# Top-32 attention with a phase mixer: the fill of the padded queries, the order of the two heads' value products, two issue orders and the folds' priority are changed

## The chip, the cores and the metric

The kernel runs on one NeuronCore of a Trainium2 chip. The metric is device time in microseconds, from one launch. The core has TensorE (PE in the profile; its weight loads are PEld), VectorE (DVE), ScalarE (ACT), GpSimd (POOL) and SyncE (SP, which here issues all transfers). Each engine works through its own list of instructions in order; a scheduler wrote these lists when the kernel was built, and semaphores tie them together.

## The reference

For 8 batches, 8 heads, 576 positions and head size 64 it computes attention that keeps the 32 largest scores of each query, and feeds the result, 512 channels wide, to a mixer:

```
scores = q @ k.T / 8
kth    = 32nd largest score of each row
attn   = softmax(where(scores >= kth, scores, -1e9))
x      = attn @ v                      # heads side by side: (8, 576, 512)
theta  = x @ w_theta
y      = w_tok_r @ (x * cos(theta)) + w_tok_i @ (x * sin(theta))
u      = x + y
out    = u + relu(u @ w_ch)
```

## The kernel before, in words

The attention is cut into 160 units: 8 batches, 4 pairs of heads each, 5 units a pair. Units j = 0 to 3 of a pair hold 128 queries of both heads; unit j = 4 holds the last 64 queries of both, which a padded tile `qpad` (zeros around two 64-column blocks) brings into one product of 128 rows. One `qpad` tile serves all 32 pairs.

A unit goes through these steps, each a function or a helper of the kernel:

- `scores` (PE L260): products of the split keys (`kh`, `kl`) with the queries into PSUM tile `ps_score` (two of them), then an ACT copy of each to `e` (L269, or L280 for j = 4). For j = 4 it first calls `pad_pair`, which fills `qpad` (L241).
- `fold` (DVE L296 to L299): maxima and minima of one half of the scores against the other; this also frees `ps_score`. `pick` (DVE L304), then `threshold` (DVE L320, L326, L330) find the 32nd largest score; POOL writes the limit `lim` (L331).
- `penalize` (ACT L350, POOL L352) and `exponent` (ACT L362) make the softmax numerators.
- `turn`: PE transposes the numerators (`pt` L377, left-over columns `pq` L387 or L391), ACT copies them to `at` (L379, L382) and `rem` (L388, L394).
- `mix_values`: for every second or so unit (j = 1 and j = 4) PE multiplies by the values into `px`: four key blocks, and in each the two heads, which go to the two halves of the output partitions (L407, 64 columns of weights each; one such product of the code is two rows of the trace), and one product for the left-over keys (L410). ACT copies the result to `xt` (L419).

After the four pairs of a batch comes its mixer, a generator that `turn` advances in small shares, so that its work lies between the next batch's units: transposes `px_s` (PE L603), normalization (DVE L502), transposes `px_t` (PE L517), the phase products `pth` (PE L540, L544), the fraction of a turn (ACT L556, DVE L557), sine and cosine (ACT L564 to L566, which need another ACT table; exponentials load theirs again at L362), the token mixing `py` (PE L656, settled by DVE L632) and the channel products `po` (PE L688, DVE L637, output L639). The last batch's mixer has nothing beside it.

The pipeline takes the steps of neighbouring units in the order PTUFKSTVMXZ, with scores and fold of unit i + 3 ahead of unit i (step S). A Tile scheduler then places every instruction by priority and readiness. Two kinds keep the order in which they are written: those that were given the token "table" (exponentials and sines on ACT) and those with the token "fixed" (on PE: `pt`, `pq` and, through `fill`, the mixer's products of all batches but the last; in the second last one the channel products are free).

At the start the weights are converted from 64-bit floats: loads L145, ACT L156, L157, L159, POOL L158, L160, L161. Each pair's keys and queries are split in two parts by ACT L212 and POOL L213 and spread by twelve transfers (L225). Values come by L232 and L235 (`vrem`, 64x64 a transfer).

Of the kernel before, what the change touches and what calls it, by code (L numbers as in the profile page):

```python
# [9 lines left out]
F32 = mybir.dt.float32  # L10
# [8 lines left out]
P = 128  # L19
# [3 lines left out]
AHEAD = 3  # L23
S_LATE = 0
# [22 lines left out]
def topk_attention_phase_mixer(  # L47
# [11 lines left out]
    nc = tc.nc  # L59
    B, NPAIR, _, S = qT.shape  # L60
    DM = w_ch.shape[0]
    D = P // 2
    H = 2 * NPAIR
    HS = S // 2
    NJ = S // P
# [22 lines left out]
    ident = const.tile([P, P], F32, name="ident")  # L88
# [85 lines left out]
    def later(n):  # L174
        return tc.high_priority(offset=-n)
# [62 lines left out]
    def pad_pair(pr):  # L238
        qpad = qpads[pr["p"] % NQP]
        for a in range(2):  # L240
            nc.scalar.copy(qpad[:, a, a * D : a * D + D], pr["q2"][:, a, NJ * P : S])  # L241
        pr["qpad"] = qpad

    class Unit:
# [152 lines left out]
    def mix_values(u):  # L397
        if u.j not in (1, NJ):
            return
        pr, bt, p = u.pair, u.batch, u.p  # L400
        c = 0 if u.j == 1 else 1
        n, q0 = QN[c], c * QN[0]
        px = ps_m.tile([P, 512], F32, tag="m", name="px")
        for kb in range(NJ):
            for a in range(2):
                sl = slice(a * D, a * D + D)
                nc.tensor.matmul(  # L407
                    px[sl, :n], pr["vt"][:, kb, sl], pr["at"][:, a, kb], start=(kb == 0), stop=False, skip_group_check=True
                )
        nc.tensor.matmul(px[:, :n], pr["vr"], pr["rem"], start=False, stop=True, skip_group_check=True)  # L410
        u.px = px
# [49 lines left out]
    def mixer(bt, split=False, beside=False, parts=False):  # L461
        bq, xt, sums, sums_rem = bt["bq"], bt["xt"], bt["sums"], bt["sums_rem"]
# [134 lines left out]
        for k in range(NJ + 4):  # L597
            if k <= NJ:
                rows = P if k < NJ else REM
                px = ps_t.tile([P, DM], F32, tag="t", name="px_s")  # L600
                with later(M_PE):
                    for p in range(NB):
                        fill(nc.tensor.transpose(px[:rows, p * P : p * P + P], xt[:, p, k * P : k * P + rows], ident))  # L603
                normalize(k, px)
            if 0 <= k - 3 <= NJ:
                fraction(k - 3)
            if 0 <= k - 2 <= NJ:
                angles(k - 2)
                yield TURN * share() / 2
            if 0 <= k - 1 <= NJ:  # L610
                turn_back(k - 1)
            yield TURN * share() / 2 if k <= NJ + 1 else 0
# [56 lines left out]
        for m in range(NB):  # L669
            if not split:  # L670
                ot = wk2.tile([P, S], F32, tag="ot", name="ot", bufs=1)
            else:
                if m % 2 == 0:
                    ots = wk2.tile([P, 2, S], F32, tag="kh", name="ots")
                ot = ots[:, m % 2]
            for c in range(2):
                cs = slice(c * HS, c * HS + HS)
                po = accumulator(m, c, "po")
                ms = slice(m * P, m * P + P)
                if split or parts:  # L680
                    mm = []
                    for kb in range(NB):
                        mm += passes(*(w[kb][:, ms] for w in w_parts["ch"]), u_hi[kb][:, cs], u_lo[kb][:, cs])
                else:
                    mm = [(wts["ch"][kb][:, ms], xt[:, kb, cs]) for kb in range(NB)]
                for i, (l, r) in enumerate(mm):
                    with later(M_TOK if split or parts else 0):
                        ins = nc.tensor.matmul(po[:, :HS], l, r, start=(i == 0), stop=(i == len(mm) - 1))  # L688
                        if not parts:
                            fill(ins)  # L690
                    if not split:
                        yield NB / len(mm)
                        flush()
                late.append(lambda m=m, c=c, cs=cs, o=ot, y=po[:, :HS]: give(m, c, cs, o, y))
                if split:
                    flush()
# [9 lines left out]
    def pipeline():  # L706
        NU = NJ + 1
        wsteps = widen_steps()
        total = B * NPAIR * NU
        units, pairs, batches, running, budget = {}, {}, {}, [], [0.0]  # L710

        def unit(i):
            if not 0 <= i < total:
                return None
            if i not in units:
                g, j = divmod(i, NU)
                b, p = divmod(g, NPAIR)
                if b not in batches:
                    batches[b] = new_batch(b)
                    if b % MARKED:  # L720
                        batches[b]["marks"] = batches[b - 1]["marks"]
                units[i] = Unit(b, batches[b], p, j, pairs[g], (g * (2 * NJ + 1) + 2 * j) % NSLOT, False)
            return units[i]

        def fetch(g):
            if g < B * NPAIR:
                pairs[g] = load_pair(*divmod(g, NPAIR))

        def split(g):
            if g < B * NPAIR:  # L730
                pairs[g] = split_pair(*divmod(g, NPAIR), pairs.get(g))

        def values(g):
            if g < B * NPAIR:
                load_values(*divmod(g, NPAIR), pairs[g])

        def advance(share):
            budget[0] = min(budget[0] + share, share) if running else 0.0
            while running and budget[0] > 0:
                with later(M_REST):  # L740
                    done = next(running[0], None)
                if done is None:
                    running.pop(0)
                else:
                    budget[0] -= done

        split(0)
        values(0)
        for i in range(AHEAD):
            scores(unit(i))  # L750
            fold(unit(i))
        pick(unit(0))
        for i in range(total + 3):
            now, nxt, old, last = unit(i), unit(i + 1), unit(i - 1), unit(i - 2)
            g, j = divmod(i, NU)
            parts = threshold(now) if now else iter(())
            pace[0] = RATE if i < total - NPAIR * NU else LAST

            def keep():
                u = unit(i - 3)  # L760
                if u:
                    keep_values(u)
                    if u.j == NJ and u.p == NPAIR - 1:
                        done = B - 1 - u.bq
                        running.append(mixer(u.batch, done == 0, done > 0, done == 1))

            def ahead():
                if unit(i + AHEAD):
                    with later(S_LATE):
                        scores(unit(i + AHEAD))  # L770
                        fold(unit(i + AHEAD))

            steps = {
                "P": lambda: old and penalize(old),
                "F": lambda: nxt and pick(nxt),
                "T": lambda: next(parts, None),
                "Z": lambda: list(parts),
                "U": lambda: last and turn(last, unit(i - 3), lambda: advance(share() / 2)),
                "K": keep,
                "S": ahead,  # L780
                "V": lambda: last and mix_values(last),
                "M": lambda: next(wsteps, None),
                "X": lambda: old and exponent(old),
            }
            for c in ORDER:
                steps[c]()
            done = unit(i - 2)
            if done and done.j == NJ and done.p == NPAIR - 1 and done.bq % MARKED == MARKED - 1:
                judge(done.batch["marks"], done.bq // MARKED)
            if i == 0:  # L790
                fetch(1)
                split(1)
            if j == 1:
                values(g + 1)
            elif j == NJ - 1:
                fetch(g + 2)
            elif j == NJ:
                split(g + 2)
        flag_f = const.tile([1, 1], F32, name="flag_f")
        nc.vector.tensor_tensor(worst, worst, kept, op=ALU.is_ge)  # L800
        nc.vector.tensor_reduce(worst[:, :1], worst, axis=AX.X, op=ALU.max)
        pf = ps_m.tile([P, 512], F32, tag="m", name="pf")
        nc.tensor.transpose(pf[:1, :P], worst[:, :1], ident)
        nc.vector.reduce_max(flag_f, pf[:1, :P], axis=AX.X)
        nc.vector.tensor_copy(flag, flag_f)
        for m in running:
            for _ in m:
                pass
# [68 lines left out]
```

## Time and profile before

| | |
|---|---|
| median of 3 runs | 1217.32 us (1216.41 to 1219.24) |
| profiled execution, its own time | 1217.33 us |
| span in its profile | 1215.2 us, 22943 instructions |
| PE busy | 1123.1 us (92%) |
| DVE busy | 1105.5 us (91%) |
| ACT busy | 1017.8 us (84%) |
| POOL busy | 704.2 us (58%) |

Busy time is the time in which an instruction of the engine ran; PE's is that of pipelined products, whose ends are modelled. The span falls in four stretches: the start (to about 38 us), the first pairs, in which TensorE's clock is below full speed and the weights are converted (to about 152 us), the steady part, in which a mixer runs beside the next batch's units (to about 1102 us, some 140 us a batch), and the last mixer. The views below are by such stretches.

### The profile page before, as it was taken

The page shows a single profiled execution, that of the slowest core. Times are in us where ns is not written, and L with a number is a line of the kernel's source. Part 1 is how long each engine was busy: PE and PEld are TensorE (multiplying, and loading weights), DVE is VectorE, ACT ScalarE, POOL GpSimd, SP SyncE. Part 2 cuts the span into 40 slices and gives each one's busy share as a digit, 9 for nine tenths or more (in the row PEclk, how much of TensorE's full clock was granted, in tenths as well). Part 3 has the DMA queues.
Part 4 walks back from the last instruction along what each step waited for, and adds up shares of the span by engine and source line. Part 5 has one row for each costly group of instructions (what it writes and reads, how often), then busy time and mean ns, then how long its engine had stood idle before and what let it go on. Part 6 is the DMA issues. An engine that isn't in the chain of part 4 may idle for free.

```text
span 1215.2 us, 22943 instructions
## 1 busy us (share of the span) xinstructions
PE 1123.1 (92%) x6325; PEld 843.9 (69%) x6325; DVE 1105.5 (91%) x4997; ACT 1017.8 (84%) x2093; POOL 704.2 (58%) x975
## 2 busy tenths in 40 slices
PE   3676779999999999999999999999999999999998
PEld 3455555777757876678757776677757777577888
DVE  7999999899999999999999999999999999997353
ACT  6899998898789988899789978898788987898561
POOL 5999865665466654666365643665465654556540
PEclk7676799999999999999999999999999999999999
DMA  6756241333423233332432234333332334200101
GB/s 173 186 161 161 78 124 31 87 89 98 118 69 89 72 91 82 97 89 69 127 88 54 67 106 108 75 91 88 112 78 56 88 99 118 69 10 11 39 2 42
DMA packets 71016, 106.11 MB, mean 87 GB/s; under 512 B 13920, under 2 KB 32608, under 8 KB 70880
## 3 DMA queue, kind: packets, MB, share of 16 engines
q1 hardware_dynamic: 70880, 104.57, 32.6%
q8 instruction: 52, 0.85, 0.3%
q14 instruction: 84, 0.69, 0.2%
HBM read 38.40 MB, written 9.44 MB: 39 GB/s over the span
## 4 chain that ended last, share of the span: by engine, by line
PE 60%; DVE 15%; ACT 14%; POOL 3%; DMA 3%; issue 2%; SPq 1%; ACTq 0%; POOLq 0%; DVEq 0%
PE py L656 18%; PE ps_score L260 9%; PE px L407 8%; PE po L688 7%; PE pt L377 7%; PE pth L540 6%; DVE lst L326 3%; DVE best L320 3%; ACT e L362 3%; DVE lst L304 3%; ACT e L269 2%; ACT pen L350 2%; PE px L410 2%; DVE lo L297 1%; SPq L225 1%
## 5 line engine op out<-in xcount | busy, mean ns | idle before, releaser
L352 POOL TENSOR_TENSOR e<-e,pen 128x576 f32<-128x576 f32 x288 | 367.0, 1289 | 138.6 <-ACT pen L350 130.8
L320 DVE MAX8 best<-lst 128x8 f32<-128x102 f32 (+3 forms) x1152 | 284.2, 291 | 12.5 <-POOL lim L331 12.0
L656 PE MATMUL py<-w,z 128*128 128x288 f32 x1008 | 267.6, 407 | 0.3 <-ACT xt L419 0.3
L362 ACT ACTIVATE e<-e,lim 128x576 f32<-128x576 f32 x288 | 225.3, 783 | 17.4 <-POOL e L352 16.5
L326 DVE MATCH_REPLACE8 lst<-best,lst 128x102 f32<-128x102 f32 (+2 forms) x864 | 232.4, 277 | 0.0
L260 PE MATMUL ps_score<-kh,q 128*128 128x288 f32 x512 | 183.8, 374 | 47.0 <-ACT e L269 22.3
L350 ACT ACTIVATE pen<-e,lim 128x576 bf16<-128x576 f32 x288 | 210.1, 776 | 9.7 <-POOL lim L331 9.5
L304 DVE MAX8 lst<-lo 128x8 f32<-128x72 f32 (+1 forms) x864 | 210.9, 296 | 0.0
L656 PEld LDWEIGHTS py<-w,z 128*128 128x128 f32 x1008 | 180.8, 190 | 40.9 <-ACT xt L419 1.6
L377 PE MATMUL pt<-ident,e 128*128 128x128 f32 x1152 | 183.5, 285 | 20.6 <-ACT e L362 15.1
L377 PEld LDWEIGHTS pt<-ident,e 128*128 128x128 f32 x1152 | 141.9, 146 | 62.1 <-ACT e L362 22.3
L269 ACT COPY e<-ps_score 128x576 f32<-128x576 f32 x256 | 162.2, 642 | 20.9 <-PE ps_score L260 18.1
L379 ACT COPY at<-pt 128x512 f32<-128x512 f32 x256 | 148.9, 590 | 27.9 <-PE pt L377 27.1
L407 PE MATMUL px<-at,vt 128*64 128x320 f32 (+1 forms) x1024 | 160.6, 426 | 2.7 <-ACT at L382 2.1
L260 PE MATMUL ps_score<-kl,q 128*128 128x288 f32 x512 | 150.6, 309 | 0.4 <-DMA kl<-raw 0.4
L260 PEld LDWEIGHTS ps_score<-kh,q 128*128 128x128 f32 x512 | 102.5, 200 | 69.3 <-ACT e L269 30.7
L407 PEld LDWEIGHTS px<-at,vt 128*64 128x64 f32 x1024 | 75.4, 141 | 64.4 <-issue 11.1
L297 DVE TENSOR_TENSOR lo<-ps_score,e 128x576 f32<-128x576 f32 (+1 forms) x160 | 110.2, 689 | 0.0
L260 PEld LDWEIGHTS ps_score<-kl,q 128*128 128x128 f32 x512 | 103.4, 202 | 6.3 <-issue 2.1
L688 PE MATMUL po<-xt,w 128*128 128x288 f32 x384 | 106.1, 407 | 0.0
L540 PE MATMUL pth<-w,xt 128*128 128x512 f32 x224 | 101.1, 594 | 0.4 <-ACT xt L518 0.4
L213 POOL TENSOR_TENSOR raw<-raw,hi 128x1152 fp32r<-128x1152 f32 x31 | 82.1, 2650 | 28.7 <-ACT hi L212 28.7
(139 smaller groups left out, 1938.4 us busy)
## 6 DMA issues: line engine op xcount, KB each, us to landing
kh<-hi SPq DMA_DIRECT2D x124, 144.0 KB, 2.8
kl<-raw SPq DMA_DIRECT2D x124, 144.0 KB, 2.8
raw<-in_qT_dram SPq DMA_DIRECT2D x31, 288.0 KB, 2.9
raw<-in_kT_dram SPq DMA_DIRECT2D x31, 288.0 KB, 3.2
q<-hi SPq DMA_DIRECT2D x62, 144.0 KB, 2.7
q<-raw SPq DMA_DIRECT2D x62, 144.0 KB, 2.9
vt<-in_v_dram SPq DMA_DIRECT2D x32, 256.0 KB, 3.3
out_dram<-ot SPq DMA_DIRECT2D x28, 288.0 KB, 2.6
```

Source lines behind the costliest of these rows:

```text
L260: nc.tensor.matmul(out[:, at : at + n], l, r, start=(i == 0), stop=(i == len(mm) - 1), skip_group_check=True)
L269: nc.scalar.copy(u.x[:, :, keys], u.ps[:, :, :HS])
L304: nc.vector.max(u.lst[:, w, QS + i * 8 : QS + i * 8 + 8], u.lo1[:, w, lo:hi])
L320: nc.vector.max(top[:, w, best], part[w])
L326: nc.vector.match_replace(out=rest, in_to_replace=top[:, w, best], in_values=part[w], imm_value=LOWEST)
L350: nc.scalar.activation(pen[:, w], u.x[:, w], AF.Relu, bias=u.lim[:, w, 0:1], scale=-STEEP)
L352: nc.gpsimd.tensor_sub(u.x[:, w], u.x[:, w], pen[:, w])
L362: nc.scalar.activation(u.x[:, w], u.x[:, w], AF.Exp, bias=u.lim[:, w, 1:2], scale=SCALE, accum_out=acc)
L377: fixed(nc.tensor.transpose(pt[:, c], e[:, w, at0 : at0 + P], ident))
L407: nc.tensor.matmul(px[sl, :n], pr["vt"][:, kb, sl], pr["at"][:, a, kb], start=(kb == 0), stop=False, skip_group_check=True)
L656: fill(nc.tensor.matmul(py[:, :HS], l, r, start=(i == 0), stop=(i == len(mm) - 1)))
L688: ins = nc.tensor.matmul(po[:, :HS], l, r, start=(i == 0), stop=(i == len(mm) - 1))
```

## The change

Five edits:

1. The two ACT copies that fill `qpad` become two transfers on SP's queue (128x64 floats each).
2. In `mix_values` the second head's product is written before the first head's in each key block.
3. The transposes `px_s` (L603) lose the token "fixed".
4. The channel products (L688) lose it too.
5. `later(S_LATE)` with S_LATE = 0 goes, and `fold` gets a priority that is higher by 200.

```
     def pad_pair(pr):
         qpad = qpads[pr["p"] % NQP]
         for a in range(2):
-            nc.scalar.copy(qpad[:, a, a * D : a * D + D], pr["q2"][:, a, NJ * P : S])
+            nc.sync.dma_start(qpad[:, a, a * D : a * D + D].bitcast(F32), pr["q2"][:, a, NJ * P : S].bitcast(F32))
...
         for kb in range(NJ):
-            for a in range(2):
+            for a in (1, 0):
...
                     for p in range(NB):
-                        fill(nc.tensor.transpose(px[:rows, p * P : p * P + P], xt[:, p, k * P : k * P + rows], ident))
+                        nc.tensor.transpose(px[:rows, p * P : p * P + P], xt[:, p, k * P : k * P + rows], ident)
...
                     with later(M_TOK if split or parts else 0):
-                        ins = nc.tensor.matmul(po[:, :HS], l, r, start=(i == 0), stop=(i == len(mm) - 1))
-                        if not parts:
-                            fill(ins)
+                        nc.tensor.matmul(po[:, :HS], l, r, start=(i == 0), stop=(i == len(mm) - 1))
...
                 if unit(i + AHEAD):
-                    with later(S_LATE):
-                        scores(unit(i + AHEAD))
+                    scores(unit(i + AHEAD))
+                    with tc.high_priority(offset=200):
                         fold(unit(i + AHEAD))
```

What this does to the engines' lists is seen in three places. The first is PE, in the token mixing of the first mixer, around the value products `px_3020` of one pair (`ps_score_3248` belongs to a unit with padded queries). Before:

```order
L387 MATMUL pq_2987<-ident_76,e_2463 128x128
L387 MATMUL pq_2987<-ident_76,e_2578 128x128
L407 MATMUL px_3020<-at0_2889,vt_2411 64x256
L260 MATMUL ps_score_3248<-kh_2699,qpad0_98 128x224
L260 MATMUL ps_score_3248<-kl_2700,qpad0_98 128x224
L260 MATMUL ps_score_3248<-kh_2699,qpad0_98 128x64
L260 MATMUL ps_score_3248<-kl_2700,qpad0_98 128x64
L407 MATMUL px_3020<-at0_2889,vt_2411 64x256 x7
L377 MATMUL pt_3054<-ident_76,e_2667 128x128 x4
```

And of the change:

```order
L260 MATMUL ps_score_3248<-kh_2699,qpad0_98 128x224
L260 MATMUL ps_score_3248<-kl_2700,qpad0_98 128x224
L260 MATMUL ps_score_3248<-kh_2699,qpad0_98 128x64
L260 MATMUL ps_score_3248<-kl_2700,qpad0_98 128x64
L407 MATMUL px_3020<-at0_2889,vt_2411 64x256 x8
L377 MATMUL pt_3054<-ident_76,e_2667 128x128 x4
```

Before, one of the eight products, the first head's first, stands ahead of the scores and the other seven behind them; now all eight stand together, where the seven stood. This is so for 22 of the 64 `px` of the pipeline before, and for none now.

The second is ACT at the end of the sines of the second mixer: `whole_4318` is the last tile of the phase, `e_4705` the scores of a unit that is three ahead, the rows with L362 are exponentials that were held back. Before:

```order
L388 COPY rem0_4211<-pq_4355 128x256
L564 ACTIVATE whole_4318<-whole_4318 128x256
L269 COPY e_4705<-ps_score_4706 128x2x288
L565 ACTIVATE whole_4318<-whole_4318 128x256
L566 ACTIVATE whole_4318<-whole_4318,half_pi_79 128x256
L362 ACT_TABLE_LOAD
L362 ACTIVATE e_3964,sums_3337<-e_3964,lim_4205 128x576 x2
L362 ACTIVATE e_4064,sums_3337<-e_4064,lim_4289 128x576 x2
L362 ACTIVATE e_4150,sums_rem_3338<-e_4150,lim_4417 128x576
L419 COPY xt_3962<-px_4388 128x256
L269 COPY e_4705<-ps_score_4712 128x2x288
```

And of the change:

```order
L388 COPY rem0_4211<-pq_4355 128x256
L564 ACTIVATE whole_4318<-whole_4318 128x256
L565 ACTIVATE whole_4318<-whole_4318 128x256
L566 ACTIVATE whole_4318<-whole_4318,half_pi_79 128x256
L362 ACT_TABLE_LOAD
L362 ACTIVATE e_3964,sums_3337<-e_3964,lim_4205 128x576 x2
L362 ACTIVATE e_4064,sums_3337<-e_4064,lim_4289 128x576 x2
L362 ACTIVATE e_4150,sums_rem_3338<-e_4150,lim_4417 128x576
L419 COPY xt_3962<-px_4388 128x256
L269 COPY e_4705<-ps_score_4706 128x2x288
L350 ACTIVATE pen_4575<-e_4248,lim_4504 128x576 x2
```

The copy of the first half of `e_4705` moved from ahead of the table load to behind the five exponentials. In the other mixers this place reads the same in both.

The third is POOL at the start, where the second pair is split (`raw_264`) while weights are converted. Before:

```order
L158 TENSOR_TENSOR room_253<-room_253,eight_81 128x512
L333 COPY marks_197<-best_142 128x2x4
L331 TENSOR_TENSOR lim_199<-best_142,factors_93 128x4
L213 TENSOR_TENSOR raw_264<-raw_264,hi_270 128x1152
L160 TENSOR_TENSOR room_253<-room_253 128x512
L352 TENSOR_TENSOR e_128<-e_128,pen_285 128x576
```

And of the change:

```order
L333 COPY marks_197<-best_142 128x2x4
L158 TENSOR_TENSOR room_253<-room_253,eight_81 128x512
L160 TENSOR_TENSOR room_253<-room_253 128x512
L331 TENSOR_TENSOR lim_199<-best_142,factors_93 128x4
L161 TENSOR_TENSOR w5_243<-room_253 128x512
L213 TENSOR_TENSOR raw_264<-raw_264,hi_270 128x1152
L352 TENSOR_TENSOR e_128<-e_128,pen_285 128x576
```

The split of the second pair moved behind a sum (L160) and a product (L161) of the conversion. Elsewhere: SP issues the two new transfers of a pair behind its twelve L225 transfers; the channel products of one half of a tile, which were broken into shares with transposes between, stand in whole groups of four.

## Rows read from the trace of the kernel before

**Rows 1.** The page: the chain that ended last, shares of the span by engine.
```profile
PE 60%; DVE 15%; ACT 14%; POOL 3%; DMA 3%; issue 2%; SPq 1%; ACTq 0%; POOLq 0%; DVEq 0%
```

**Rows 2.** Windows by stage: busy time of each engine, granted clock, DMA.
```profile
core 0: us, PE busy (x) PEld busy (x) DVE busy (x) ACT busy (x) POOL busy (x), PEclk, DMA share, GB/s
...
38.00:152.00 114.00, 84.07 (x402) 61.53 (x400) 109.83 (x536) 110.25 (x226) 104.21 (x131) 0.72 0.50 142
152.00:1102.00 950.00, 919.21 (x5165) 678.20 (x5166) 914.94 (x4209) 823.36 (x1705) 532.23 (x773) 1.00 0.33 85
...
484.90:764.50 279.60, 273.92 (x1545) 202.83 (x1544) 269.87 (x1244) 240.68 (x500) 155.53 (x226) 1.00 0.34 88
575.00:611.00 36.00, 35.54 (x216) 26.94 (x215) 36.00 (x166) 26.07 (x54) 15.14 (x23) 1.00 0.43 124
```

**Rows 3.** DVE's waits from 152 to 1102 us: total, times, longest.
```profile
DVE best L320 <- POOL lim L331: 12.0, 6, 2.6
DVE ps_score L296 <- ACT e L269: 6.1, 10, 1.5
DVE xt L632 <- PE py L656: 6.1, 9, 1.4
```

**Rows 4.** The chain from 484.9 to 764.5 us: start, length, what.
```profile
488.30 0.68 PE px L407 x2
489.24 2.30 PE px L407 x14
...
526.88 2.30 PE px L407 x16
...
540.38 0.58 PE px L407 x2
...
541.68 1.87 PE px L407 x14
...
576.52 1.88 PE px L407 x16
```

**Rows 5.** PE's timeline: the first and the last of 22 such rows.
```profile
85.53 0.65 PE L407 MATMUL px<-at,vt 128*64 128x256 f32 x2
...
1049.79 0.75 PE L407 MATMUL px<-at,vt 128*64 128x320 f32 x2
```

**Rows 6.** DVE's timeline: three of its waits.
```profile
371.42 0.27 DVE L320 MAX8 best<-lst 128x8 f32<-128x102 f32 x1 [2.58 <-POOL lim L331]
...
546.12 0.46 DVE L632 TENSOR_TENSOR xt<-py,xt 128x288 f32<-128x288 f32 x1 [0.90 <-PE py L656]
...
549.31 0.47 DVE L296 TENSOR_TENSOR ps_score<-ps_score,e 128x288 f32<-128x288 f32 x1 [0.74 <-ACT e L269]
```

**Rows 7.** ACT's instructions of line 241: duration ns min/median/max, first and last start.
```profile
L241 ACT CAST qpad<-q x64: 230/246/329, 10.9 to 1061.9; 128x64 fp32r<-128x64 f32 x64
```

**Rows 8.** Start of the program: POOL's timeline, then one piece of the chain.
```profile
25.13 1.30 POOL L161 TENSOR_TENSOR w<-room 128x512 f32<-128x512 f32 x1
...
27.77 2.63 POOL L213 TENSOR_TENSOR raw<-raw,hi 128x1152 fp32r<-128x1152 f32 x1
30.35 1.26 POOL L160 TENSOR_TENSOR room<-room 128x512 int32<-128x512 int32 x1
...
34.85 4.20 DMA kl<-raw
```

**Rows 9.** ACT's timeline at the end of the second mixer's sines.
```profile
366.67 0.63 ACT L269 COPY e<-ps_score 128x576 f32<-128x576 f32 x1
...
373.54 0.63 ACT L269 COPY e<-ps_score 128x576 f32<-128x576 f32 x1
374.07 1.45 ACT L350 ACTIVATE pen<-e,lim 128x576 bf16<-128x576 f32 x2
```

**Rows 10.** SP's instructions of line 235: issue ns, and us to landing.
```profile
L235 SPq DMA_DIRECT2D vrem<-in_v_dram x64: 472/574/1542, 5.4 to 1096.3; - x64
...
DMA to landing us min/median/max: 1.9/2.7/4.3
```

## The prediction

> **What bounds the kernel now.** I read the page's chain first: it names the engine whose work or waits led to the end. PE holds 60% of it, DVE and ACT 14 to 15% each [rows 1]. Averages over stages mislead, so next the windows. From 38 to 152 us DVE (109.83 of 114.00) and ACT (110.25) are both full and PE is not (84.07). From 152 to 1102 us PE is busy 919.21 and DVE 914.94 of 950.00: both some 97%, so each has only 31 and 35 us of idle time, and no edit can give more there than what the later of the two leaves [rows 2]. In two batches, 279.6 us, DVE idles 9.73 us, 4.9 a batch. The channel products' stretch has no idle time on DVE at all (36.00 of 36.00) and half a microsecond on PE. What does DVE wait for in its 35 us? For POOL's limit 12.0 us in six waits (the exponentials held back by the sines have to be done first), for `py` of PE 6.1 us, for the score copies 6.1 us [rows 3]. So behind DVE's idle time stand stages that PE paces: the end of the phase products and the token mixing.
>
> **The value products (edit 2).** This is the largest term. In the chain a whole group of value products, 16 rows, takes 1.88 us for 256 queries and 2.30 us for 320. Where the first head's first product was put ahead, its two rows take 0.58 or 0.68 us, and the other 14 rows still take 1.87 or 2.30 us [rows 4]. The two heads' products run over each other (they fill different output halves); the one put ahead has no partner, and at the end the second head's last has none. So putting it ahead costs 0.58 + 1.87 - 1.88 = 0.57 us, or 0.68 us for 320. It happens in 22 of 64 groups; the first is at 85.53, the last at 1049.79 us [rows 5]. The reason is in the code: the first head's numerators are turned first, so its product is ready first and the scheduler takes it as a filler. Written second head first, nothing of the group is ready before all is, and the order of the change has no split group.
>
> The Trainium skill (TensorEngine Tiling (Array Packing), Key Properties) states that different tiles can execute weight loads and matmuls in parallel. The trace agrees. By its rule alone a lone product would cost one quarter of the group, 0.47 or 0.58 us as an estimate, and the gain below would be a sixth smaller.
>
> Two of the 22 lie ahead of 152 us, where PE has room: worth nothing. Of the 20 behind, 13 have 256 queries and 7 have 320: 13 x 0.57 + 7 x 0.68 = 12.2 us less work on PE. Followed one by one, 16 of them lie on the chain (9 of 256, 7 of 320; two are in [rows 4]): 9 x 0.57 + 7 x 0.68 = 9.9 us. Is there room on DVE for it? The split at 540.31 is followed at 546.12 by a wait of 0.90 us for `py` and at 549.31 by one of 0.74 us for scores [rows 6]; each batch's other two lead to the phase products and then to the wait for the limit, up to 2.58 us [rows 6]. About 1.5 us a batch against 4.9 us idle: it fits. I take **-9.9**; bounds -4 (only the seven in front of a `py` wait count) and -12.2.
>
> **Padded queries by transfers (edit 1).** It removes 64 ACT copies of 0.246 us, 16 us in all [rows 7]. In the steady part ACT has over 13% idle time and none of the copies is on the chain: 0. From 38 to 152 us ACT is full; seven copies lie there, at most 7 x 0.33 = 2.3 us, and DVE idles just 4.2 us in it [rows 2]. I take **-1.0**; bounds 0 and -2.3. The transfers themselves: two issues of about 0.57 us on SP per pair and a landing of 2.7 us, at most 4.3, by the nearest row, transfers half that size [rows 10]. They stand behind the pair's twelve split transfers, and the padded unit is the fifth of its pair, a good 25 us later; they wait for the preceding pair's padded products to let go of the one tile, and behind them in the queue are loads for a pair one or two further on. The attention units are the cover: 0. Without it each pair would pay 2.7 us in place of 0.25 (rival c).
>
> The Trainium skill speaks against this edit: DMA: Bandwidth & Descriptors, Rules for kernel authors, says that transfers under 64 KB are mostly overhead, and these are 32 KB. The landing rows agree; the same table says to issue early and wait late.
>
> **The start.** Here the order changes for the worse. POOL's split of the second pair, which began at 27.77 us, comes behind one L160 (1.26 us) and one L161 (1.30 us): 2.5 us later [rows 8]. One of the older transfers that stood between its six is issued earlier and gives about 0.6 us back, and the key transfer that follows is on the chain (4.20 us at 34.85). The first two `qpad` transfers also stand ahead of a weight load, which has room. I take **+1.7**; bounds 0 (DVE's waits in the next stage absorb it) and +2.5.
>
> **Second mixer's sines (edit 5 and the scheduler's answer).** The score copy at 366.67 us goes behind five exponentials; what followed it, the table load, comes 0.53 us earlier, while the unit's second copy, at 373.54, comes behind another copy and two L350 (1.45 us) [rows 9]: 0.63 + 1.45 + 0.63 - 0.53, some 2.2 us for the fold, which waits there already. I take **+1.7**; bounds -0.5 (the 2.58 us wait shortens and the fold is covered by thresholds) and +2.2.
>
> **Channel products, `px_s`, folds (edits 3 to 5).** Instruction counts don't change on PE and DVE. Where the channel products now come in whole groups, scores of units ahead come up to 20 matmuls later, but in a stretch in which DVE has a backlog (36.00 of 36.00 [rows 2]): 0. The higher priority leaves folds at about the same places, a row or two later on average, since a fold can't stand ahead of its scores. Bounds for all three: -2 (the products' results leave earlier) and +8 (waits for score copies, 6.1 us in ten now [rows 3], more than double). I take 0.
>
> **The sum.** -9.9 - 1.0 + 1.7 + 1.7 = -7.5 us. The profiled execution took 1217.33 us, 0.01 above the median: 1209.8, say **1210 us**. All low ends together give -18 us or so, all high ends about +9.
>
> **Rivals.** (a) DVE becomes the bound at once. For it: DVE has as little idle time as PE, and past some channel products the chain already runs along it. Then a freed microsecond on PE turns into a wait of PE for `ps_score`, a third or so of the 9.9 us arrives, and the start and the sines take it: 1217.3 - 3.3 - 1.0 + 3.4 = 1216.4. Against it: the waits of DVE named above lie directly behind the splits.
>
> (b) The other side: scores come late and folds wait. Scores stand about five matmuls later on average; in the mixing stage, where PE has no slack, that is about 1 us. Three new waits of 0.9 us a batch over seven batches are +19 us; less 9.9, and with the start and the sines, 1217.3 + 19 - 7.5 = 1229. It decides from 1.1 us of new fold waits a batch (7.5 / 7). Half the price gives 1219. Against it: three units are in flight, and only ten fold waits over 0.1 us stand in the steady part now.
>
> (c) The transfers show. If the padded scores waited a full landing, 32 x (2.7 + 0.6 - 0.25) = 98 us; far from it with 25 us of cover, but a tenth of the pairs would cost 10 us and end at 1220. Coverage has to fall below about 4 us. The rule of the DMA page named above would make it so only for a transfer issued right before its use.
>
> (d) More than the sum: the freed PE time and the whole groups also remove waits for scores and limits; a third more of DVE's 35 us goes: 1217.3 - 7.5 - 10 = 1200.
>
> **Chances.** My forecast 0.56 (own range 1205 to 1214), (a) 0.17, (b) 0.10, (c) 0.05, (d) 0.12. 2.4 us, 0.2%, is about what a measurement tells from no change. Faster: nearly all of the forecast, (d), and a fifth of (a): 0.70. Same: most of (a) and a little of the rest, 0.15. Slower: (b) and (c), 0.15. The range, 1202 to 1220, leaves out the far ends of (b) and (d).
>
> **What would show it.** In the changed profile no value group with two rows apart, 16 rows in 1.88 or 2.30 us everywhere, PE's work behind 152 us about 12 us less; waits for `py` near 3 us in place of 6.1, for the limit near 8; no L241 on ACT; POOL's first L213 near 30 us and DVE's fold of the sixth unit near 44. I would be wrong if DVE's idle time from 152 us on stayed at 35 us although the groups are whole (a), if the waits of L296 for score copies rose beyond 14 us (b), or if PE waited for `qpad` (c).

## The result and the profile after

The changed kernel takes 1201.82 us (1201.61 to 1202.05, 4 runs) against 1218.28 us (1216.41 to 1220.37, 4 runs): ratio 0.9869, 95% interval 0.9854 to 0.9883, 16.5 us faster. The forecast was 1210 and its range reached down to 1202, where the measured time lies: the sign was right and the gain about twice as large as forecast.

The page of the changed kernel, the chain by engine. PE held 60% before [rows 1]; part of it went over to DVE:

```profile
PE 49%; DVE 24%; ACT 17%; POOL 5%; issue 2%; DMA 2%; SPq 1%; ACTq 0%; DVEq 0%; POOLq 0%
```

The windows by stage (the steady part ends 14 us earlier than in [rows 2]):

```profile
core 0: us, PE busy (x) PEld busy (x) DVE busy (x) ACT busy (x) POOL busy (x), PEclk, DMA share, GB/s
38.00:152.00 114.00, 81.61 (x396) 57.65 (x394) 107.66 (x521) 106.47 (x213) 101.84 (x125) 0.75 0.52 147
152.00:1088.00 936.00, 904.65 (x5180) 678.12 (x5181) 915.42 (x4226) 818.24 (x1661) 535.85 (x778) 1.00 0.34 88
```

Read DVE's column: 915.42 us of work in 936, where it was 914.94 in 950. The work is the same; its idle time fell from 35.1 to 20.6 us, and these 14.5 us are nearly the whole gain in the span (14.9 us, 1215.2 to 1200.3). What DVE still waits for from 152 to 1088 us (total, times, longest):

```profile
DVE ps_score L296 <- ACT e L269: 8.6, 13, 1.2
DVE best L320 <- POOL lim L331: 7.8, 6, 2.1
DVE end L502 <- PE px_s L603: 0.8, 1, 0.8
DVE ps_score L296 <- ACT e L280: 0.6, 3, 0.2
```

One row of the same view of the kernel before, beside those of [rows 3]:

```profile
DVE z L557 <- ACT whole L556: 3.6, 5, 1.2
```

The 6.1 us for `py` of [rows 3] are gone, those for the limit fell from 12.0 to 7.8, and those for the fraction (L557) from 3.6 to nothing. The waits for score copies did not fall (8.6 for 6.1). So of the forecast's signs of being wrong none came: DVE's idle time did not stay at 35 us (a), the score waits did not pass 14 us (b), and PE never waited for `qpad` (c). PE's work behind 152 us is 14.6 us less (904.65 for 919.21), where about 12 was forecast.

In the chain of two batches no value group is split any more; three of its nine groups, to be set beside [rows 4]:

```profile
522.85 2.30 PE px L407 x16
...
536.87 1.88 PE px L407 x16
...
560.48 2.30 PE px L407 x16
```

At the start POOL's split of the second pair begins 2.0 us later than in [rows 8], as forecast:

```profile
29.79 2.63 POOL L213 TENSOR_TENSOR raw<-raw,hi 128x1152 fp32r<-128x1152 f32 x1
```

But the fold that hangs on it, at 42.34 us before with a wait of 2.08, comes earlier, not later; and the wait for the limit behind the second mixer's sines is 0.70 us where [rows 6] has 2.58. DVE's timeline:

```profile
41.13 0.47 DVE L296 TENSOR_TENSOR ps_score<-ps_score,e 128x288 f32<-128x288 f32 x1 [1.15 <-ACT e L269]
...
369.94 0.27 DVE L320 MAX8 best<-lst 128x8 f32<-128x102 f32 x1 [0.70 <-POOL lim L331]
```

And the padded queries' transfers, 64 issues on SP (compare [rows 10]):

```profile
L241 SPq DMA_DIRECT2D qpad<-q x64: 475/496/821, 10.9 to 1045.6; - x64
...
DMA to landing us min/median/max: 1.7/1.8/3.6
```

### The profile page after: what moved, and what is told of

Same layout as the page of the kernel before. It is cut to its first block, busy times and chain, and to the rows that moved or that the text cites. A ratio compares the mean times of both kernels' runs of the same rounds, so it can differ in the third digit from the quotient of the medians.

```text
span 1200.3 us, 23013 instructions
## 1 busy us (share of the span) xinstructions
PE 1104.9 (92%) x6325; PEld 839.3 (70%) x6325; DVE 1102.9 (92%) x4997; ACT 1007.0 (84%) x2029; POOL 704.4 (59%) x975
## 4 chain that ended last, share of the span: by engine, by line
PE 49%; DVE 24%; ACT 17%; POOL 5%; issue 2%; DMA 2%; SPq 1%; ACTq 0%; DVEq 0%; POOLq 0%
PE py L656 15%; PE ps_score L260 6%; PE po L688 6%; PE pt L377 6%; PE px L407 6%; DVE lst L326 5%; PE pth L540 5%; DVE best L320 5%; DVE lst L304 4%; ACT e L362 4%; ACT pen L350 3%; ACT e L269 3%; DVE lo L297 2%; PE px L410 1%; DVE ps_score L296 1%
## 5 line engine op out<-in xcount | busy, mean ns | idle before, releaser
L656 PE MATMUL py<-w,z 128*128 128x288 f32 x1008 | 267.9, 407 | 0.3 <-ACT xt L419 0.3
L362 ACT ACTIVATE e<-e,lim 128x576 f32<-128x576 f32 x288 | 225.1, 783 | 18.0 <-POOL e L352 17.2
L326 DVE MATCH_REPLACE8 lst<-best,lst 128x122 f32<-128x122 f32 (+2 forms) x864 | 231.4, 274 | 0.1
L656 PEld LDWEIGHTS py<-w,z 128*128 128x128 f32 x1008 | 181.1, 191 | 40.2 <-ACT xt L419 1.2
L377 PE MATMUL pt<-ident,e 128*128 128x128 f32 x1152 | 181.0, 283 | 23.0 <-ACT e L362 14.9
L269 ACT COPY e<-ps_score 128x576 f32<-128x576 f32 x256 | 161.8, 641 | 15.2 <-PE ps_score L260 14.7
L407 PE MATMUL px<-at,vt 128*64 128x320 f32 (+1 forms) x1024 | 145.1, 428 | 1.7 <-ACT at L382 1.3
L407 PEld LDWEIGHTS px<-at,vt 128*64 128x64 f32 x1024 | 70.8, 143 | 55.5 <-issue 10.2
L688 PE MATMUL po<-xt,w 128*128 128x288 f32 x384 | 100.4, 408 | 0.0
```

Of the source, the lines that this page charges most:

```text
L269: nc.scalar.copy(u.x[:, :, keys], u.ps[:, :, :HS])
L326: nc.vector.match_replace(out=rest, in_to_replace=top[:, w, best], in_values=part[w], imm_value=LOWEST)
L362: nc.scalar.activation(u.x[:, w], u.x[:, w], AF.Exp, bias=u.lim[:, w, 1:2], scale=SCALE, accum_out=acc)
L377: fixed(nc.tensor.transpose(pt[:, c], e[:, w, at0 : at0 + P], ident))
L407: nc.tensor.matmul(px[sl, :n], pr["vt"][:, kb, sl], pr["at"][:, a, kb], start=(kb == 0), stop=False, skip_group_check=True)
L656: fill(nc.tensor.matmul(py[:, :HS], l, r, start=(i == 0), stop=(i == len(mm) - 1)))
```

## The experiments

Twelve kernels ran. The theories at the outset: A, the forecast's, that split value groups cost what they take on PE; B, that the free order of `px_s` and the channel products counts; C, that the folds' priority does. D came after the first four runs.

**One edit alone, on the kernel before.** Second head first only:

```
-            for a in range(2):
+            for a in (1, 0):
```

> The kernel before with the second head's value products written first, and nothing else. Theory A (a value group that is split costs 0.57 to 0.68 us of TensorE, and 16 of the 20 late ones lie on the chain): 8 to 12 us faster, no row of two value products left, waits of VectorE for py fall from 6.1 us to under 3. Theory B (the free order of px_s and the channel products is what counts): under 4 us faster. Theory C (the folds' priority counts): under 2 us faster.

Measured 1224.42 us against 1218.21: ratio 1.0059 (1.0046 to 1.0073), slower. No theory had that. (The profile is of an execution of 1219.19 us; five of the seven took 1224.24 to 1225.81, and what these lost besides, no trace shows.) The waits for `py` did go, but for one of 2.5 us at 852.65 us, and from the fifth sine block on (762.51 us) to the last (1159.06) it gains 4.2 us on the kernel before. The loss lies ahead of that: at 515.96 us, where the third mixer's sines end, it was 8.3 us behind. The windows show what goes with it (PEclk, the granted clock, is the third column from the end). The first row is the kernel before, the other two are this run:

```profile
152.00:200.00 48.00, 39.13 (x232) 27.18 (x233) 48.00 (x225) 44.78 (x99) 27.09 (x42) 1.00 0.35 90
...
152.00:200.00 48.00, 39.33 (x208) 28.09 (x207) 46.59 (x227) 43.87 (x97) 28.73 (x45) 0.79 0.32 84
...
490.00:494.00 4.00, 4.00 (x19) 3.82 (x20) 2.71 (x17) 3.92 (x8) 2.86 (x4) 0.59 0.08 19
```

TensorE's granted clock was 0.79 on average from 152 to 200 us and 0.59 from 490 to 494; the kernel before has 1.00 in both stretches. That the clock cost the 8.3 us is an argument: no run changes the clock alone. Ahead of the second fall stands a wait of PE:

```profile
490.00 0.69 PE L387 MATMUL pq<-ident,e 128*128 128x128 f32 x2 [2.69 <-ACT at L379]
```

The transfers only:

```
-            nc.scalar.copy(qpad[:, a, a * D : a * D + D], pr["q2"][:, a, NJ * P : S])
+            nc.sync.dma_start(qpad[:, a, a * D : a * D + D].bitcast(F32), pr["q2"][:, a, NJ * P : S].bitcast(F32))
```

> The kernel before with the padded queries filled by transfers, and nothing else. Theory A: 0 to 3 us faster, all of it before 152 us, where ScalarE is full; its order has 20 split value groups of 72 where before had 24, which would give another 2 us. If the copies cost the steady part too (each holds up ScalarE's queue behind TensorE's padded products): 5 us or more faster. If the transfers show: slower by several us, with TensorE waiting for qpad.

1223.81 us, ratio 1.0053 (1.0040 to 1.0067), slower, though PE does not wait for `qpad` here either and the landing is the same 1.8 us. Waits for score copies rose to 15.2 us, and four stretches at half clock (1.2 GHz; the granted clock falls to 0.5 there) lie behind 150 us.

The free order only (`px_s` and channel products without `fill`):

```
-                        fill(nc.tensor.transpose(px[:rows, p * P : p * P + P], xt[:, p, k * P : k * P + rows], ident))
+                        nc.tensor.transpose(px[:rows, p * P : p * P + P], xt[:, p, k * P : k * P + rows], ident)
...
-                        if not parts:
-                            fill(ins)
```

> The kernel before with px_s and the channel products free of the given order, and nothing else. Its order has 12 split value groups of 72 where before had 24. Theory A: half of the splits' cost, 5 us faster, no more. Theory B: 8 us or more faster, with the gain lying in the channel products' and the phase products' stretches.

1235.32 us, ratio 1.0144 (1.0128 to 1.0159): 17 us slower, against B and A. DVE's waits from 152 us to the last mixer are the late scores of the forecast's rival (b), and late channel products, which it did not have:

```profile
DVE ps_score L296 <- ACT e L269: 24.4, 31, 2.0
DVE ot L637 <- PE po L688: 10.6, 5, 3.0
DVE xt L632 <- PE py L656: 9.1, 10, 1.8
```

Its phase products show what half clock costs. Two groups of eight in PE's timeline, the same work; the granted clock was 1.00 in the first and 0.68 on average in the second, which stands behind a wait of 2.28 us:

```profile
765.31 3.60 PE L540 MATMUL pth<-w,xt 128*128 128x512 f32 x8
...
777.24 5.40 PE L540 MATMUL pth<-w,xt 128*128 128x512 f32 x8 [2.28 <-ACT xt L518]
```

The folds' priority only:

```
-                    with later(S_LATE):
-                        scores(unit(i + AHEAD))
-                        fold(unit(i + AHEAD))
+                    scores(unit(i + AHEAD))
+                    with tc.high_priority(offset=200):
+                        fold(unit(i + AHEAD))
```

> The kernel before with the folds at a higher priority, and nothing else; 25 split value groups. Theory A and B: within 2 us. Theory C: 4 us or more faster, and VectorE's waits for score copies (7.8 us from 152 us on) fall.

1217.45 us, ratio 0.9997 (0.9987 to 1.0008): no difference, as A and B had it; C is out as a cause by itself.

Edits of which three alone make the kernel slower and one changes nothing give 16.5 us together. So theory D: each edit makes the scheduler place many instructions anew, and a run of one edit measures that placement as well, above all where PE waits around the sines and whether its clock falls there. D allows any time from 1200 to 1235 us, so a time in that range is no proof of it, and no run parts placement from an edit's own price.

**One edit undone, on the changed kernel.** The first head first again:

```
-            for a in (1, 0):
+            for a in range(2):
```

> The changed kernel with the first head's value products first again; its order has 18 split groups of 72. Theory A (each late split costs its 0.57 to 0.68 us, as the forecast has it): 8 to 12 us slower than the change, 1210 to 1214 us. Theory D (what the single edits cost or give is set by where the scheduler's answer leaves TensorE without work around the sines, and whether its clock falls there): the split prices are there, but the total may be anywhere from 1200 to 1235, and goes with the number of stretches at half clock behind 150 us, about 3 us each (before 2, change 2 early ones).

1229.70 us against 1218.13: ratio 1.0096 (1.0080 to 1.0113), 28 us slower than the change. Without this edit the whole gain is lost and more. (So it is without the free `px_s` alone, below: the edits are not parts of one sum.) The splits are back in the chain:

```profile
604.48 0.57 PE px L407 x2
...
606.26 1.87 PE px L407 x14
```

and with them DVE's waits for `py`, while those for score copies more than double:

```profile
DVE ps_score L296 <- ACT e L269: 21.2, 31, 2.2
DVE xt L632 <- PE py L656: 9.9, 12, 2.1
DVE ot L637 <- PE po L688: 5.7, 4, 2.6
```

28 us is three times A's price, and only some 3 us more loss at half clock stand beside it, so the rest stays open.

ScalarE's copies again (the transfers' diff reversed):

```
-            nc.sync.dma_start(qpad[:, a, a * D : a * D + D].bitcast(F32), pr["q2"][:, a, NJ * P : S].bitcast(F32))
+            nc.scalar.copy(qpad[:, a, a * D : a * D + D], pr["q2"][:, a, NJ * P : S])
```

> The changed kernel with the padded queries filled by ScalarE copies again; no split groups. Theory A: 1 us slower, all of it before 152 us, 1201 to 1204. Theory D: anywhere from 1200 to 1235, with the number of stretches at half clock; the alone run of the transfers was 5.6 us slower, so if the edit has a price of its own this one is 5 us faster, near 1196.

1210.09 us, ratio 0.9935 (0.9918 to 0.9952): 8 us slower than the change, where alone the transfers cost 6. So it shows no price of its own that holds in both places. Much of 150 to 190 us is at half clock here (0.74 on average, the change 0.96).

The given order for both `px_s` and the channel products:

```
-                        nc.tensor.transpose(px[:rows, p * P : p * P + P], xt[:, p, k * P : k * P + rows], ident)
+                        fill(nc.tensor.transpose(px[:rows, p * P : p * P + P], xt[:, p, k * P : k * P + rows], ident))
...
+                        if not parts:
+                            fill(ins)
```

> The changed kernel with px_s and the channel products in the given order again; no split groups. Theory A: as fast as the change, within 2 us. If the edit has a price of its own (alone it was 17 us slower): 1185 to 1190. Theory D: its harm comes only with value groups that can be split or with ScalarE's copies in the way, so with the other edits kept it is worth nothing or a gain: 1202 to 1215.

1213.83 us, ratio 0.9963 (0.9951 to 0.9975), 12 us slower than the change.

The folds at the old priority:

```
-                    with tc.high_priority(offset=200):
-                        fold(unit(i + AHEAD))
+                    fold(unit(i + AHEAD))
```

> The changed kernel with the folds at the old priority; one group of 72 is split. Theory A and the run of the folds alone (no difference): 1200 to 1204. Theory D: anywhere from 1200 to 1235, with the number of stretches at half clock.

1207.68 us, ratio 0.9913 (0.9896 to 0.9929), 6 us slower. It falls 8 us behind between the second and the third sine block (142.0 us from table load to table load, the change 134.1), and from the third to the seventh it is as fast (547.8 against 549.4): one place, not the folds at large.

**What the head order does.** All four products of one head first, so that no neighbours belong to different heads:

```
-        for kb in range(NJ):
-            for a in (1, 0):
+        for a in (1, 0):
+            for kb in range(NJ):
```

> The changed kernel with all four value products of the second head first, then all four of the first: the two heads no longer alternate. If the two heads' products run over each other only as neighbours (the forecast's reason for the price of a split): a group of 16 rows takes about 3.7 and 4.6 us in place of 1.88 and 2.30, 32 x 1.88 + 32 x 2.30 = 134 us more work on TensorE, of which 90 to 134 us show: 1290 to 1335 us. If they do not overlap, and a split costs for another reason (a restart of the pipeline): 16 rows still in 1.9 and 2.3 us, 1200 to 1210 us.

1255.28 us against 1217.24, ratio 1.0305 (1.0289 to 1.0320), between the two ranges expected. PE's timeline, whole groups:

```profile
504.74 3.50 PE L407 MATMUL px<-at,vt 128*64 128x320 f32 x16
508.17 0.40 PE L260 MATMUL ps_score<-kh,q 128*128 128x288 f32 x1
...
522.48 2.86 PE L407 MATMUL px<-at,vt 128*64 128x256 f32 x16
525.27 0.70 PE L410 MATMUL px<-rem,vrem 128*128 128x256 f32 x2
```

From start to next start a group takes 3.43 and 2.79 us in place of 2.30 and 1.88. So alternating heads do run over each other, but not as fully as expected: a product of 256 queries costs 0.35 us alone (2.79 / 8) and 0.235 us in the alternation (1.88 / 8). The extra work, 32 x 0.91 + 32 x 1.13 = 65 us, shows as 53.5 us against the change: 82% of what is put on PE appears in the time, if the placements are alike otherwise.

The traces also take the price of a split apart. The kernel before has two groups that are broken in the middle, between whole pairs of products; this run has one from which a product is split off, with no partner to lose. PE's timeline, first before, then this run:

```profile
737.78 1.30 PE L407 MATMUL px<-at,vt 128*64 128x320 f32 x8
739.01 0.66 PE L603 MATMUL px_s<-ident,xt 128*128 128x128 f32 x4
739.59 1.30 PE L407 MATMUL px<-at,vt 128*64 128x320 f32 x8
740.82 0.81 PE L410 MATMUL px<-rem,vrem 128*128 128x320 f32 x2
...
331.79 2.43 PE L407 MATMUL px<-at,vt 128*64 128x256 f32 x14
334.15 0.66 PE L517 MATMUL px_t<-ident,z 128*128 128x128 f32 x4
334.74 0.65 PE L407 MATMUL px<-at,vt 128*64 128x256 f32 x2
335.31 0.40 PE L260 MATMUL ps_score<-kh,qpad 128*128 128x288 f32 x1
```

From start to next start these are 1.23 + 1.23 - 2.30 = 0.16 us and 2.36 + 0.57 - 2.79 = 0.14 us. A split that breaks the alternation costs 0.57 or 0.68 us. So some 0.15 us of that is the break itself and the rest the partner that is lost, as the forecast had it.

The second head first in the first block only:

```
-            for a in (1, 0):
+            for a in (1, 0) if kb == 0 else (0, 1):
```

> The changed kernel with the second head first in the first key block only; the three others have the first head first. No group is split in its order. If all that the second edit does is to keep a group whole: no waits of VectorE for py, the same 1.88 and 2.30 us a group, and net of stretches at half clock as fast as the change, 1198 to 1210 us. If the order of the heads in each block counts: 1210 to 1230 us, like the run with the first head's products first.

1214.65 us (1208.72 to 1217.56), ratio 0.9973 (0.9959 to 0.9987). DVE's waits up to the last mixer have no row for `py`:

```profile
DVE best L320 <- POOL lim L331: 13.0, 7, 2.4
DVE ps_score L296 <- ACT e L269: 8.4, 14, 1.4
DVE end L502 <- PE px_s L603: 3.5, 2, 2.2
```

All its groups take 1.88 and 2.30 us. Its median lies in the range that was expected if the order of the heads in each block counts; net of six stretches at half clock behind 150 us it is at 1198.6, as expected if only whole groups count. So the reading that only whole groups count rests on that column. One stretch is the window from 484 to 488 us, behind a wait of 2.22 us for `at` at 482.64:

```profile
484.00:488.00 4.00, 4.00 (x7) 1.63 (x6) 4.00 (x18) 4.00 (x9) 2.86 (x4) 0.57 0.33 71
```

**Which of the freed orders.** `px_s` alone in the given order again, then the channel products alone:

```
-                        nc.tensor.transpose(px[:rows, p * P : p * P + P], xt[:, p, k * P : k * P + rows], ident)
+                        fill(nc.tensor.transpose(px[:rows, p * P : p * P + P], xt[:, p, k * P : k * P + rows], ident))
```

> The changed kernel with px_s alone in the given order again. If the free channel products bring what edits 3 and 4 bring together (12 us in the run with both back): 1200 to 1204 us. If px_s does: 1210 to 1214 us. If what that run lost was stretches at half clock alone (5.7 + 4.6 us of TensorE's time against 3.2 in the change): the time goes with these, wherever they come.

```
-                        nc.tensor.matmul(po[:, :HS], l, r, start=(i == 0), stop=(i == len(mm) - 1))
+                        ins = nc.tensor.matmul(po[:, :HS], l, r, start=(i == 0), stop=(i == len(mm) - 1))
+                        if not parts:
+                            fill(ins)
```

> The changed kernel with the channel products alone in the given order again. If the free channel products bring what edits 3 and 4 bring: 1210 to 1214 us. If px_s does: 1200 to 1204 us. If only half clock counts: the time goes with the stretches at half clock; span less TensorE's loss from them stays at 1195 to 1200 us, as in the change (1197).

1224.00 us (ratio 1.0051, 1.0039 to 1.0063) and 1213.89 us (0.9973, 0.9963 to 0.9983). With both in the given order it was 1213.83: giving back `px_s` alone costs 22 us, the channel products alone 12, both 12, so their effects don't add. The first has nine stretches at half clock behind 150 us, one in each of seven mixers' sines, and 17.9 us of waits for score copies. Half clock does not explain all of it: net of that it is still 12 us behind the change, with only three groups split.

**All runs side by side.** "Split" counts the value groups behind 152 us from which a product without its partner stands apart; "py" and "scores" are DVE's waits of L632 for L656 and of L296 for L269 from 152 us to 120 us before the end; "half clock" sums, over windows of 2 us from 150 us to 113 us before the end, PE's busy time times one less the granted clock; the last column is the span less that. The times are medians, all else is of the one profiled execution (values only 1219.2 us, px_s back 1228.6, the others within 2.2 us of their medians). The run with the heads apart is left out: its value products alone are 65 us more.

| run | us | split | py | scores | half clock | span less it |
|---|---|---|---|---|---|---|
| before | 1218.3 | 20 | 6.1 | 6.1 | 3.2 | 1212.0 |
| transfers only | 1223.8 | 18 | 5.0 | 15.2 | 9.6 | 1212.4 |
| free order only | 1235.3 | 10 | 9.1 | 24.4 | 13.7 | 1220.0 |
| folds only | 1217.5 | 20 | 6.2 | 6.3 | 3.1 | 1214.3 |
| values back | 1229.7 | 16 | 9.9 | 21.2 | 6.1 | 1220.4 |
| values only | 1224.4 | 1 | 2.5 | 8.2 | 13.2 | 1204.2 |
| change | 1201.8 | 0 | 0 | 8.6 | 3.2 | 1197.1 |
| copies back | 1210.1 | 0 | 0 | 10.2 | 10.5 | 1197.3 |
| order back | 1213.8 | 0 | 0.4 | 11.7 | 10.3 | 1202.0 |
| folds back | 1207.7 | 1 | 0 | 9.9 | 6.4 | 1199.4 |
| first block swapped | 1214.7 | 0 | 0 | 8.4 | 12.6 | 1198.6 |
| px_s back | 1224.0 | 3 | 0.3 | 17.9 | 17.4 | 1209.4 |
| channel products back | 1213.9 | 0 | 1.9 | 10.4 | 7.7 | 1203.1 |

(The five groups that are split with the second head first stand in pieces of three and five products. Such a group of 320 queries takes 1.22 + 1.76 us, 0.68 more than a whole one, like the others.)

The last column parts the runs without overlap, by 2.6 us: 1212 to 1220 us with the first head first (five runs), 1197 to 1209 with groups that start with the second (eight runs). So do the waits for `py`: 5.0 to 9.9 us against 0 to 2.5. The column is rough, since not every microsecond that PE loses to its clock lies on the path, and since it has one execution of each kernel, while those of the first block swapped spread from 1208.7 to 1217.6 us.

## Why the prediction was right in sign and short in size

**Value products.** Right in its mechanism: no split group is left in the change, 1.88 and 2.30 us everywhere, no wait for `py` (at most 2.5 us in the kernels that have the edit with others undone), and neighbours of different heads shown to run over each other. The step that came out too small is its term, "-9.9" with the bound "-12.2". Net of half clock the edit alone gives 1212.0 - 1204.2 = 7.8 us, which A's price covers; within the other edits 1220.4 - 1197.1 = 23 us. The forecast had each edit priced by itself and added; this one changes what the others are worth. What the 23 us are beyond some 10 us for 16 splits (10 at 0.57, 6 at 0.68 us) is not shown; beside them stand score waits of 21.2 us for 8.6 and waits for channel products of 5.7 us for none.

Of the rivals (d) came nearest, 1200 us: the waits for the limit did shrink, as it says; those for scores, which it names too, did not.

**Channel products and `px_s`, taken as 0.** Wrong. With the first head first, freeing them costs: 17 us measured, 8 net, beside late score copies, as in rival (b), and late channel products. With the second head first it gains: 12 us measured, 5 net. The backlog of DVE in the channel products' stretch, which was to hide late scores, did not hide them when value groups were split. Why a group that can be split and a free order get in each other's way is not settled: both give the scheduler loose pieces to put in front of scores, but no run shows that step, and freeing one of the two alone did not sort out which matters.

**Padded queries.** The transfers are hidden as forecast: landing 1.8 us, no wait of PE, and net of half clock nothing either way (1212.4 against 1212.0; 1197.3 against 1197.1). The 6 us that they cost alone and the 8 us that they gain within the change are both about what the half clock column shows (9.6 for 3.2; 10.5 for 3.2), not the copies' 16 us. The rule against small transfers of the Trainium skill (DMA: Bandwidth & Descriptors, Rules for kernel authors), named in the forecast, did not show as a cost here: these land in 1.8 us, and PE waits for none of them.

**The start, "+1.7".** Wrong in the part behind POOL. The split came 2.0 us later and the key transfers behind it were issued 0.8 to 1.4 us later, but they landed in 2.7 us where the one in the chain of before has 4.20 [rows 8]. The same four transfers among those issued from 30 to 40 us, before and in the change (KB each, median us to landing):

```profile
kl<-raw SPq DMA_DIRECT2D x4, 144.0 KB, 4.3
...
kl<-raw SPq DMA_DIRECT2D x4, 144.0 KB, 2.7
```

In the order of the change the next weight load and the next pair's loads, 288 to 576 KB each, stand on SP behind the two `qpad` transfers and come later; the 16 DMA engines were 85% busy from 30 to 40 us, where before it was 99%. That these loads had held up the keys is an argument from these rows, no run tests it. The fold came 1.2 us earlier, not 1.7 later.

**Second mixer's sines, "+1.7".** Wrong. The score copy did go behind five exponentials (372.06 for 366.67 us), but the fold is not waited for: DVE has thresholds to work on, since the table load comes 2.8 us earlier, counted from the block's first table load (28.3 us behind it for 31.1), and with it the wait for the limit shrinks (0.70 for 2.58 us). The lower bound gave just these two reasons, a shorter wait for the limit and thresholds that cover the fold; taking +1.7 instead was the step that failed here.

**What was not in the sum.** Half clock. The kernel before loses 3.2 us of PE behind 150 us and the change 3.2, so it does not explain the gain; but other runs lose up to 14 us of PE time more, and by the table's last column it hid the main effect in the run of that edit alone. In the kernel before PE's wait of 2.22 us at 1042.54 stands ahead of such a stretch, and the last sine block of the steady part, 34.9 us there, takes 31.5 in the change.

**The sum's bounds.** The low ends that the forecast gives add up to -17.0 us, not "-18 or so"; this changes nothing above.

## What to carry to other kernels

Where two products share the array by halves, write first the one whose data comes last, so that a scheduler cannot take its partner away as a filler; look in the trace for small groups that take as long as their rest. In a kernel that a scheduler places, an edit alone and the same edit within others can be worth quite different amounts (here 6 us slower alone, 28 us faster within the rest): measure both, and read per-stage waits and the granted clock before the total. A gain of two engines that are both 97% busy is read from the idle time of the one whose work did not change.

## What the hardware showed that was not expected

Products of 64 columns of weights for different halves of the output cost 0.235 us in alternation and 0.35 us alone (256 queries), so the overlap saves a third, not a half. Splitting one off costs 0.57 us, breaking a group between pairs 0.16 us (320 queries). After waits of PE of 2.2 to 2.7 us around the sines the granted clock fell to 0.57, 0.59 and 0.68 in the windows named above, mixtures of 2.4 and 1.2 GHz, and the same eight phase products took 5.40 us in place of 3.60. Not every such wait is followed by a fall: with the folds at the old priority in the changed kernel PE waits 2.80 us at such a place, up to 487.04 us, and the granted clock is 1.00 from 487 to 497 us.
